# A planned order of all engines' work, replanned with a later landing of crossbar transposes, with new leads and offsets

## The chip, the cores and the metric

The kernel runs on one core of a Trainium2 chip. The metric is the device time of one execution in microseconds (us). Three runs of the kernel before took 236.09, 234.23 and 234.80 us, so the median is 234.80 us. A core has five engines that run side by side and each take their instructions in the order in which the program lists them: TensorE (PE, matrix products, with weight loads as PEld), VectorE (DVE), ScalarE (ACT), GpSimd (POOL) and SyncE (SP). POOL and SP compute nothing here: they issue transfers.

## The reference

For 8 batches of 576 positions, attention with 8 heads of 64 elements, in a sliding window of 128 positions with a linear position bias, and then a channel mix on its 512-wide result. In numpy, cut to what matters:

```python
scores = where((rel >= 0) & (rel < 128), q @ k.T / 8 - slope[h] * abs(rel), -1e9)
x = softmax(scores) @ v                       # heads side by side: (8, 576, 512)
x_prev = x shifted down by one position, zeros first
xk = mu_k * x + (1 - mu_k) * x_prev
xr = mu_r * x + (1 - mu_r) * x_prev
out = sigmoid(xr @ w_r) * (relu(xk @ w_k) ** 2 @ w_v)    # w_k 512x1024, w_v 1024x512
```

## The kernel before

**The work.** Positions lie in tiles of 128 (four and a half a batch), heads in four pairs g = 0 to 3. For every batch b and pair g the steps are:

- Transposed queries and keys. For batches 0 to 5 TensorE makes them (`qk_quad`, `qk_some`, lines 1053 and 804) and ScalarE or VectorE copies them out of PSUM (line 663). For batches 6 and 7 (`XB`) SyncE issues eight crossbar transposes for each batch (`flip`, line 502, tile `qx` from `cb`). The last 64 positions of batches 4 to 7 come by one more (`tail_flip`, line 595, `tt` from `ts`).
- Scores (`scores`, line 693, a contraction over 64 rows), the exponential on ScalarE (line 707, `at`), and the mask as a product on VectorE (line 720).
- Attention times values (`attend`, line 749, `duo`), the reciprocal of the sum (line 755) and the scaled result `xu` (line 760) on VectorE.
- The result transposed to `xt`: on TensorE for batches 0 to 5 (`out_t`, `out_some`, lines 787 and 804), by crossbar transposes from SyncE for batches 6 and 7 (`out_flip`, line 869, `xt` from `xu`).
- On VectorE the difference to the position before, `dl` (line 847), and the two mixtures `xk` and `xr` (line 854), in `shift`.

The channel mix then runs over groups of columns of two batches together, 512, 384 and 256 wide (`channel_mix`): eight products with `wk_sb` (line 958), each followed by a relu on ScalarE (line 965, `rl`) and a square on VectorE or ScalarE (lines 931 and 929, `kk`); and for each tile of 128 positions four matmuls with `wr_sb` (line 976), a tanh on ScalarE (line 983, `rs`), two halves of four matmuls with `wv_sb` (line 992), one VectorE instruction (line 997, `ot`), and a store from SyncE (line 1022). All of these, and the TensorE transposes, share four PSUM banks, `uno`; scores and most attention products use two double banks, `duo`.

**The order.** Nothing of the order is left to a scheduler at run time. The program describes every operation as a node with its engine, duration, delay to its followers, and the buffers it takes and gives back. `Plan.run` then plays all engines forward and, whenever an engine is free, gives it the ready node with the smallest key. The order that comes out is the order of the program. These constants feed it:

- `FLAT`: two delays of a crossbar transpose, between its issue and the start of its transfer, and from the end of its transfer to the time when its data may be used. `flip`, `tail_flip` and `out_flip` pass it on.
- `WAIT`: added to the key of a TensorE node marked lazy (transposes that use the array in halves of 64 rows) as long as the array is in its 128-row form.
- `LEAD` and `SHIFT`: an attention node's key is `(k - lead(e, k)) * SLOPE + SHIFT`, where k counts batches and pairs. `lead` interpolates the ten numbers of an engine, one for every fourth k. A larger lead puts the attention of that stretch earlier against the channel mix on that engine. A mix node's key is its own place plus a `SHIFT` by the buffers it takes and frees.

The four lines with the delay of a crossbar transpose, at the issue in `flip` and where the delays are used:

```python
        return dma(SPE, FLIP * RATE, FISSUE, lambda e: nc.sync.dma_start_transpose(
            ...
            [g, (cl[b][NF * i + j], FWAIT)], (), [ch[b]], FLAT, True)
        ...
        n0, edge = n, (n, lat[0])                       # in fab
            x = plan.add(FAB, us / m, lat[1] if i == m - 1 else 0.0, [edge], ...)
```

Of the kernel before, what the change touches and what calls it, by code (L numbers as in the profile page):

```python
# [182 lines left out]
def kernel(  # L183
# [29 lines left out]
    PE, ACT, DVE, POOL, SPE, FAB, VIR = "PE", "ACT", "DVE", "POOL", "SP", "FAB", "VIR"  # L213
# [15 lines left out]
    RUN = {2: 64 * 284 / 345.0, NF: 128 * 284 / 390.0}  # L229
    FLIP = 1.0  # L230
    FISSUE = 1.3
    FLAT = (0.4, 0.6)
    FWAIT = 6.0
    NO = 5
    WAIT = 3.32
    COST = {'first': 1.28, 'v': 1.15, 'q': 0.944, 'ts': 0.66, 'tv': 0.58, 'w': 0.88, 'run4': 1.0, 'run2': 1.03, 'flip': 1.0, 'mu': 1.0, 'x': 1.0}
    SS = ()
    OH = range(1, 6)
# [77 lines left out]
    def two(h):  # L316
# [3 lines left out]
                     xk=2, rl=3, kk=3, rs=4, ot=NO),  # L320
                {}, WAIT)
    LAT = {PE: 0.2, ACT: 0.22, DVE: 0.16}
# [7 lines left out]
    def dve_t(n, fast=1):  # L330
# [1 line left out]

    AHEAD = 30.0
    LEAD = {
        PE: (20.71, 45.98, 25.48, 22.48, 33.7, 13.57, 16.34, 19.02, 18.98, 21.49),
        ACT: (-12.8, -31.96, 26.95, -42.55, -38.86, -42.12, 50.62, -66.43, -27.26, -47.28),
        DVE: (-9.64, -23.6, -20.1, 21.59, -38.02, 19.17, 21.38, -10.6, -61.51, -15.57),
    }
    KNOTS = range(-4, 36, 4)
    SHIFT = {  # L340
        PE: {(0, 0): 75.8, (1, 0): 3.7, (2, 0): 53.98, (3, 0): 68.58, ('fkk',): -70.0, ('p1', 'fkk'): 14.4, ('p1', 'fxk'): 15.56},
        ACT: {(1, 0): -100.8, (2, 0): 67.78, (3, 0): 84.72, ('frl',): 15.27, ('rl', 'fp1'): 97.76, ('rs', 'fp1'): -101.33},
        DVE: {(0, 0): -161.9, (1, 0): 90.77, (1, 1): -32.45, (1, 2): -60.98, (2, 0): 28.48, (3, 0): -12.21, ('fp1', 'frs'): -33.9, ('frl',): -130.25, ('ot', 'fp1', 'frs'): -5.67},
    }
    NBIAS = 4
    XRL = 4.0
# [34 lines left out]
    def fab(queue, us, n, lat, free=(), flip=False):  # L381
        m = max(1, round(us / 0.25))
        us *= COST.get(getattr(n, "kind", None), 1.0)
        n0, edge = n, (n, lat[0])
        for i in range(m):
            x = plan.add(FAB, us / m, lat[1] if i == m - 1 else 0.0, [edge], (0,), None, (),
                         free if i == m - 1 else ())
            x.queue, x.base, x.flip = queue, n0, flip
            edge = (x, 0.0)
        return x  # L390
# [110 lines left out]
    def flip(b, i, j, g):  # L501
        return dma(SPE, FLIP * RATE, FISSUE, lambda e: nc.sync.dma_start_transpose(
            out=qx_buf[xbh[b].idx][:, i, :, 128 * j:128 * j + 128],
            in_=cb_buf[ch[b].idx][:, i, j].rearrange("p h d -> p (h d)")),
            [g, (cl[b][NF * i + j], FWAIT)], (), [ch[b]], FLAT, True)

# [84 lines left out]
    def tail_flip(b):  # L591
# [5 lines left out]
            in_=ts_buf[hs.idx].rearrange("p h d -> p (h d)")),  # L597
            [g] + [(x, FWAIT) for x in tl[b]], (), [hs], FLAT, True)]

# [266 lines left out]
    def out_flip(b, g, r, hx, ht):  # L866
# [4 lines left out]
            in_=xu_buf[hx.idx].rearrange("p t h d -> p (t h d)")))  # L871
        return [fab(SPE, FLIP * NJ / 4, n, FLAT, [hx], True)]

# [427 lines left out]
```

## Time and profile before

| | |
|---|---|
| median of three runs | 234.80 us |
| the profiled execution's own time | 233.99 us |
| its span, first to last instruction | 232.2 us |
| PE busy | 222.9 us, 96% |
| DVE busy | 187.7 us, 81% |
| ACT busy | 165.4 us, 71% |
| crossbar transposes `qx` from `cb` | 16, median 5.9 us from issue to landing |
| crossbar transposes `xt` from `xu` | 8, median 3.7 us |
| crossbar transposes `tt` from `ts` | 4, median 2.5 us |

The profile is of one execution. Its span is 1.8 us shorter than that execution's own time, which lies outside the first and the last instruction. The busy time of PE is the time in which at least one matmul is under way; matmuls follow each other before the one ahead has ended, so durations overlap, and the distance between the starts of two matmuls is what one costs.

### The profile page before, as it was taken

How to read it: one execution, taken by the hardware profiler on the slowest of the kernel's cores; microseconds unless marked ns; L12 is line 12 of the kernel's file. 1: busy time of each engine (PE TensorE's matmuls, PEld its weight loads, DVE VectorE, ACT ScalarE, POOL GpSimd, SP SyncE). 2: the span in 40 equal slices, each digit the busy share in tenths (PEclk: the TensorE clock that was granted, in tenths of full speed). 3: DMA queues.
4: the chain of work that ended last, by engine and by line, in shares of the span. 5: the costliest groups of instructions: out<-in, count | busy, mean ns of one | idle time of the engine just before them, and what ended most of it. 6: DMA issues, size and time to landing. Idle time of an engine off the chain costs nothing.

```text
span 232.2 us, 6668 instructions
## 1 busy us (share of the span) xinstructions
PE 222.9 (96%) x2687; PEld 135.2 (58%) x2715; DVE 187.7 (81%) x422; ACT 165.4 (71%) x296; POOL 93.9 (40%) x120
## 2 busy tenths in 40 slices
PE   8999799999999999999999999999998999999994
PEld 8676665765665755555665755555646644445462
DVE  7495899899868999879779997999989899624242
ACT  3769999699997985968998847478775636236261
POOL 8796654689977940097400992600000000000000
PEclk9999999999999999999999999999999999999999
DMA  7999999999999997089994999999412712121212
GB/s 171 184 167 193 187 170 199 204 165 178 168 165 146 168 156 139 0 96 173 211 149 113 153 143 194 142 183 197 54 51 90 110 54 74 47 91 45 93 45 90
DMA packets 121566, 31.11 MB, mean 134 GB/s; under 512 B 108216, under 2 KB 117696, under 8 KB 121536
## 3 DMA queue, kind: packets, MB, share of 16 engines
q0 software_dynamic: 96016, 16.26, 98.5%
q1 hardware_dynamic: 23776, 13.84, 26.2%
q10 hardware_dynamic: 1744, 0.59, 1.0%
q8 instruction: 21, 0.34, 0.7%
q14 instruction: 9, 0.07, 0.1%
HBM read 33.56 MB, written 9.44 MB: 185 GB/s over the span
## 4 chain that ended last, share of the span: by engine, by line
PE 74%; DVE 12%; DMA 7%; ACT 3%; issue 2%; POOL 1%; DVEq 0%; ACTq 0%
PE uno L992 22%; PE uno L958 20%; PE uno L976 11%; PE duo L749 6%; DMA wv_sb<-in_moe_w_v_dram 5%; PE duo L693 5%; PE uno L654 3%; PE uno L804 2%; DVE ot L997 2%; DMA xt<-xu 2%; DVE xr L854 2%; DVE dl L847 2%; DVE xk L854 2%; DVE at L720 2%; PE duo L680 1%
## 5 line engine op out<-in xcount | busy, mean ns | idle before, releaser
L992 PE MATMUL uno<-wv_sb,kk 128*128 128x512 bf16 (+2 forms) x277 | 70.4, 373 | 1.5 <-issue 0.3
L958 PE MATMUL uno<-xk,wk_sb 128*128 128x256 bf16 (+2 forms) x410 | 69.3, 313 | 0.9 <-ACT qk L663 0.4
L707 ACT ACTIVATE at<-duo 128x1024 bf16<-128x1024 f32 (+2 forms) x68 | 65.6, 1014 | 5.4 <-PE duo L693 5.3
L965 ACT ACTIVATE rl<-uno 128x256 bf16<-128x256 f32 (+2 forms) x104 | 48.1, 489 | 20.9 <-PE uno L958 16.5
L958 PEld LDWEIGHTS <-wk_sb 128*128 128x128 bf16 x416 | 38.4, 98 | 21.0 <-issue 1.6
L467 POOL DMA_DIRECT2D vs<-in_v_dram x32 | 28.4, 901 | 45.1 <-PE duo L749 37.9
L992 PEld LDWEIGHTS <-kk 128*128 128x128 bf16 x296 | 27.1, 98 | 29.5 <-issue 1.3
L720 DVE TENSOR_TENSOR at<-at,mask 128x1024 bf16<-128x1024 bf16 x56 | 37.0, 684 | 7.5 <-ACT at L707 7.3
L983 ACT ACTIVATE rs<-uno 128x512 bf16<-128x512 f32 x36 | 22.2, 624 | 24.5 <-PE uno L976 23.6
L976 PE MATMUL uno<-wr_sb,xr 128*128 128x512 bf16 x141 | 36.5, 379 | 1.1 <-DVE ot L997 0.9
L997 DVE SCALAR_TENSOR_TENSOR ot<-rs,uno 128x512 f32<-128x512 bf16 (+2 forms) x37 | 24.6, 667 | 15.3 <-PE uno L992 13.0
L931 DVE TENSOR_TENSOR kk<-rl 128x256 bf16<-128x256 bf16 (+2 forms) x96 | 31.0, 338 | 6.5 <-ACT rl L965 5.2
L663 ACT COPY qk<-uno 128x512 bf16<-128x512 bf16 (+1 forms) x42 | 22.8, 601 | 4.6 <-DVE rc L755 2.1
L854 DVE SCALAR_TENSOR_TENSOR xr<-dl,mu_sb,xt 128x576 bf16<-128x576 bf16 (+1 forms) x32 | 24.5, 775 | 0.0
L854 DVE SCALAR_TENSOR_TENSOR xk<-dl,mu_sb,xt 128x576 bf16<-128x576 bf16 (+1 forms) x32 | 24.3, 778 | 0.0
L749 PEld LDWEIGHTS <-at 128*128 128x128 bf16 x576 | 21.1, 98 | 5.1 <-issue 0.9
L976 PEld LDWEIGHTS <-xr 128*128 128x128 bf16 x144 | 13.9, 98 | 17.0 <-issue 0.9
L760 DVE TENSOR_TENSOR xu<-duo,rc 128x640 bf16<-128x640 f32 x28 | 22.5, 812 | 0.9 <-DMA xt<-xu 0.8
L498 POOL DMA_DIRECT2D cb<-in_k_dram x20 | 17.8, 920 | 2.6 <-DMA vs<-in_v_dram 1.6
L749 PE MATMUL duo<-vs,at 128*128 128x65 bf16 x448 | 18.7, 194 | 0.1
L498 POOL DMA_DIRECT2D cb<-in_q_dram x20 | 17.7, 922 | 1.4 <-PE uno L958 0.7
L663 ACT COPY xt<-uno 128x640 bf16<-128x640 bf16 (+3 forms) x28 | 15.0, 582 | 4.2 <-PE uno L804 2.8
(83 smaller groups left out, 201.3 us busy)
## 6 DMA issues: line engine op xcount, KB each, us to landing
out_dram<-ot SPq DMA_DIRECT2D x30, 256.0 KB, 4.5
vs<-in_v_dram POOLq DMA_DIRECT2D x32, 128.0 KB, 6.8
cb<-in_q_dram POOLq DMA_DIRECT2D x20, 128.0 KB, 6.3
cb<-in_k_dram POOLq DMA_DIRECT2D x20, 128.0 KB, 6.4
out_dram<-ot SPq DMA_DIRECT2D x10, 128.0 KB, 1.8
wk_sb<-in_moe_w_k_dram POOLq DMA_DIRECT2D x2, 512.0 KB, 7.4
cb<-in_q_dram POOLq DMA_DIRECT2D x4, 256.0 KB, 10.0
cb<-in_k_dram POOLq DMA_DIRECT2D x4, 256.0 KB, 10.3
```

What stands on the lines that cost most here:

```text
L498: return [dma(POOL, 256, issue_t(1024), lambda e, r=r: nc.gpsimd.dma_start(out=cb_buf[h.idx][:, i, r], in_=src[:, :, r]), [g], kind="q") f ...
L663: (nc.scalar.copy if e == ACT else nc.vector.tensor_copy)(out=out, in_=in_)
L707: lambda e, ah=ah, w=w, hp=hp: nc.scalar.activation(out=ah(), in_=two(hp)[:, :, 0:w], func=AF.Exp, scale=float(scale)), (), [hp])
L720: nc.vector.tensor_tensor(out=a, in0=a, in1=m, op=ALU.mult)
L749: nc.tensor.matmul(a[:, hl, t - t0], lhsT=at[:, lo:lo + 128], rhs=vs[:, u, 2 * g + hl, :] if u < NF else tvb[:, 2 * g + hl], start=(u == u ...
L854: lambda e: nc.vector.scalar_tensor_tensor(out=buf[hk.idx][:, g, e0 + c0:e0 + c1], in0=dls(), scalar=mu[:, g:g + 1], in1=xc(1), op0=ALU.mu ...
L931: nc.vector.tensor_tensor(out=out, in0=in_, in1=in_, op=ALU.mult)
L958: nc.tensor.matmul(one(hp)[:, 0:n], lhsT=wk_sb[:, po, 128 * fo:128 * fo + 128], rhs=xk_buf[hx.idx][:, po, c0:c1], start=(po == 0), stop=(p ...
L965: a = op(ACT, act_t(n), [s], pr, lambda e, hp=hp, hr=hr: nc.scalar.activation(out=rl_buf[hr.idx][:, 0:n], in_=one(hp)[:, 0:n], func=AF.Rel ...
L976: nc.tensor.matmul(one(hp), lhsT=xr_buf[hx.idx][:, po, 128 * c:128 * c + 128], rhs=wr_sb[:, po], start=(po == 0), stop=(po == NPO - 1))
L992: nc.tensor.matmul(one(hv)[:, a:b], lhsT=kk_buf[hk.idx][:, fo, o:o + 128], rhs=wv_sb[:, fo, a:b], start=(fo == 0), stop=(fo == NFO - 1))
L997: nc.vector.scalar_tensor_tensor(out=ot_buf[ho.idx][:, a:b], in0=rs_buf[hs.idx][:, a:b], scalar=1.0, in1=one(hv)[:, a:b], op0=ALU.add, op1 ...
```

## The change

Four sets of constants are replaced. The second delay in `FLAT` goes from 0.6 to 2.2 us, `WAIT` goes from 3.32 to 0.0, and the tables `LEAD` and `SHIFT` get new numbers. No function is changed, no operation is added or taken away, and the buffers are the same. The order in which `Plan.run` lists the operations of PE, ACT, DVE and SP is another. The order of POOL is the same.

```diff
-    FLAT = (0.4, 0.6)
+    FLAT = (0.4, 2.2)
     FWAIT = 6.0
     NO = 5
-    WAIT = 3.32
+    WAIT = 0.0
...
     LEAD = {
-        PE: (20.71, 45.98, 25.48, 22.48, 33.7, 13.57, 16.34, 19.02, 18.98, 21.49),
-        ACT: (-12.8, -31.96, 26.95, -42.55, -38.86, -42.12, 50.62, -66.43, -27.26, -47.28),
-        DVE: (-9.64, -23.6, -20.1, 21.59, -38.02, 19.17, 21.38, -10.6, -61.51, -15.57),
+        PE: (46.3, 80.42, 22.29, 25.79, 41.56, 20.38, 22.23, 21.29, 23.26, 26.51),
+        ACT: (-27.56, -45.55, 35.23, -5.26, -38.06, -61.17, 26.65, -81.7, -33.31, -34.13),
+        DVE: (-18.77, -31.64, -26.58, 23.63, -67.49, 40.6, 13.9, -0.29, -44.69, 6.99),
     }
...
     SHIFT = {
-        PE: {(0, 0): 75.8, (1, 0): 3.7, (2, 0): 53.98, (3, 0): 68.58, ('fkk',): -70.0, ('p1', 'fkk'): 14.4, ('p1', 'fxk'): 15.56},
-        ACT: {(1, 0): -100.8, (2, 0): 67.78, (3, 0): 84.72, ('frl',): 15.27, ('rl', 'fp1'): 97.76, ('rs', 'fp1'): -101.33},
-        DVE: {(0, 0): -161.9, (1, 0): 90.77, (1, 1): -32.45, (1, 2): -60.98, (2, 0): 28.48, (3, 0): -12.21, ('fp1', 'frs'): -33.9, ('frl',): -130.25, ('ot', 'fp1', 'frs'): -5.67},
+        PE: {(0, 0): 84.89, (1, 0): -15.49, (2, 0): 37.21, (3, 0): 68.05, ('fkk',): -41.42, ('p1', 'fkk'): 6.29, ('p1', 'fxk'): 4.19},
+        ACT: {(1, 0): -163.12, (2, 0): 31.31, (3, 0): 165.14, ('frl',): 21.61, ('rl', 'fp1'): 159.69, ('rs', 'fp1'): -160.42},
+        DVE: {(0, 0): -143.93, (1, 0): 53.57, (1, 1): -50.21, (1, 2): -15.35, (2, 0): 32.09, (3, 0): -4.67, ('fp1', 'frs'): -48.4, ('frl',): -99.03, ('ot', 'fp1', 'frs'): -1.01},
     }
```

## Prediction

> **What bounds the kernel now.** I read the page first, then the waits of PE, then the order of time around each wait.
>
> ```profile
> PE 222.9 (96%) x2687; PEld 135.2 (58%) x2715; DVE 187.7 (81%) x422; ACT 165.4 (71%) x296; POOL 93.9 (40%) x120
> ...
> PEclk9999999999999999999999999999999999999999
> ...
> PE 74%; DVE 12%; DMA 7%; ACT 3%; issue 2%; POOL 1%; DVEq 0%; ACTq 0%
> ```
>
> PE is busy for 96% of the span, at full granted clock in each slice, and is three quarters of the chain that ended last. Whether a busy PE is a full PE is told by the starts of its matmuls, in the timeline of PE (start, duration, line, shapes, count):
>
> ```profile
> 154.63 1.03 PE L976 MATMUL uno<-wr_sb,xr 128*128 128x512 bf16 x4
> 155.49 1.03 PE L992 MATMUL uno<-wv_sb,kk 128*128 128x512 bf16 x4
> 156.45 0.56 PE L693 MATMUL duo<-qx 64*128 64x256 bf16 x8
> 156.85 0.19 PE L693 MATMUL duo<-tt,qx 64*128 64x64 bf16 x2
> 156.88 0.19 PE L693 MATMUL duo<-tt 64*128 64x64 bf16 x2
> 157.00 1.04 PE L992 MATMUL uno<-wv_sb,kk 128*128 128x512 bf16 x4
> ```
>
> Four matmuls 512 wide take 0.86 us (155.49 less 154.63), 0.216 each, and the next four follow at once: this stretch is full. The four ahead of the scores take 0.96: the change to the 64-row form costs 0.10 us, and the change back about as much (0.12 us for two matmuls that cost some 0.03 together). In the sum a change costs 0.095.
>
> What PE waits for, in the view of its waits (us in total, times, longest):
>
> ```profile
> PE uno L879 <- ACT qk L663: 1.2, 1, 1.2
> PE uno L654 <- DVE warm L434: 1.0, 1, 1.0
> PE uno L976 <- DVE ot L997: 0.9, 1, 0.9
> PE uno L958 <- ACT qk L663: 0.4, 1, 0.4
> ```
>
> By the timeline the first, second and fourth lie ahead of 45 us. The third, at 175 us, is the only long one behind that. The rest there is short: 0.1 to 0.15 us each, about 0.4 in all. It matters where they lie because, by the orders of the two programs, PE lists the same instructions until about 47 us; up to there ACT and DVE each exchange two neighbours. So the change can win back some 1.3 us of waits between 47 us and the last matmul at 229.2, and no more. The 3.0 us from there to the end of the span, the last VectorE step and the stores, have the same operations in both.
>
> **The wait that goes.** In the timelines of DVE and PE:
>
> ```profile
> 169.18 0.46 DVE L847 TENSOR_TENSOR dl<-xt 128x576 bf16<-128x576 bf16 x1 [0.98 <-DMA xt<-xu]
> ...
> 174.65 0.68 DVE L997 SCALAR_TENSOR_TENSOR ot<-rs,uno 128x512 f32<-128x512 bf16 x1
> ```
>
> ```profile
> 175.38 1.02 PE L976 MATMUL uno<-wr_sb,xr 128*128 128x512 bf16 x4 [0.88 <-DVE ot L997]
> ```
>
> DVE stood 0.98 us for a crossbar transpose of batch 6, with all its later work behind it; 6 us later L997 gave a bank back late, and PE stood 0.88 us. What covers such a transpose is the DVE work listed between the multiplication that makes `xu` (L760) and the subtraction that reads `xt` (L847). Counted for the eight transposes with the rows' distances (L720, L997 0.60; L760, L854 0.73; L847 0.37; L931 0.21 to 0.33; L755 0.13 to 0.2), it is 5.1, 3.6, 5.4, 4.6, 3.3, 8.0, 7.0 and 3.9 us before, and 5.6, 7.3, 4.9, 12.6, 5.3, 5.9, 5.0 and 6.3 after. The transposes land in 2.4 to 4.9 us, median 3.7. The second, with 3.6 us of cover, is the one that was late (4.5). After, the least cover is 4.9. So the wait goes: **-0.88 us**. What is late next there is PE itself: the rows of L958 follow.
>
> **What is added.** The operations and their durations are the same, so PE's sum changes only by changes of form. Counted in the two orders there are 98 before and 102 after (lazy transposes no longer wait for 3.32 in the key): 4 x 0.095 = **+0.38 us**, all on the path. Matmul work, warm-up included, is 222.2 us before and 222.6 after. The Trainium skill has a rule for this, in "TensorEngine Tiling (Array Packing)": a change of tiling mode, not of tile, drains the array. The trace agrees, with 0.10 us a change; the page gives no price, and by it too the new order is the dearer one.
>
> The order on ACT and DVE costs nothing where PE has other work ahead of what waits for it. At the end it has: 40.7 us of matmul work after the last attention product, 38.1 before, and between that product and the first L958 that needs its mixtures 16.4 us in both, against some 8 us for L755, L760, transpose, L847 and four L854. The exchange on ACT near 17 us (an exponential ahead of a 0.3 us copy) is made good by the next instruction: nothing.
>
> **What is brought nearer.** The first scores of batch 7 have 161.5 us of matmul work ahead before and 155.5 after: six us earlier. They started at 166.64, so 5.1 us were lost by then. They read `qx`, all eight transposes, and `tt`. SP's timeline before (its queue in order), and the landings of `qx`:
>
> ```profile
> 138.41 11.50 SPq L502 DMA_TRANSPOSE qx<-cb  x7
> 150.75 0.34 SPq L1022 DMA_DIRECT2D out_dram<-ot  x1
> 151.18 1.30 SPq L502 DMA_TRANSPOSE qx<-cb  x1
> 152.65 1.24 SPq L595 DMA_TRANSPOSE tt<-ts  x1
> ```
>
> ```profile
> DMA to landing us min/median/max: 2.5/5.6/8.2
> ```
>
> The last `qx` was issued at 151.2 and landed by 159.4 at the latest, 7 us ahead of need. After, SP lists one transpose, then a store, then seven, then `tt`. That store's mix has 136.0 us of matmul work up to its end. The two stores ahead of the transposes before had 129.5 and 132.1 and were issued at 137.4 and 138.0, 5.9 to 7.9 us later on the clock. So the store goes at 141.8 to 143.8. Seven transposes at the row's 1.64 us: the last starts at 151.7 to 153.7 and lands, at the median, at 157.3 to 159.3, at the worst at 161.9; `tt` is issued at 153.3 to 155.3 and lands with its own 2.5 us by 157.8, with the worst of `qx` by 163.5. Needed: 155.5 + 5.1 = 160.6. The cost is between nothing and 2.9 us. I take nothing, as the medians stay 1.3 us clear. What waits behind the scores, if they are late, is all of PE.
>
> For batch 6 the same count (scores at 130.4 + 4.9 = 135.3; the six transposes behind the store with 105.5 us start near 112, and are through by 121) leaves over 6 us.
>
> **The sum.** 233.99 (the profiled execution: span 232.2 and 1.8 around it) - 0.88 + 0.38 = 233.5. The shown runs have a median 0.8 us above this execution; from them the sum is 234.3. I take the middle, **233.9 us**. One per cent, 2.35 us, is about what a measurement of this kernel can tell from no change.
>
> **The rivals.**
> 1. *The transposes of batch 7 come too late* (slower than before). Place: the first L693 of batch 7. It decides when the last of them lands more than 160.6 us into the span. For it: `qx` took up to 8.2 us beside the loads, 2.5 at the least, and in the new order the last attention product of batch 5, for which POOL's loads of `vs` wait, comes 3.5 us of work later, so these loads fall on the transposes. Against it: the earlier loads, of `cb`, come 1.8 us sooner, and the median is clear. Price up to 2.9: 233.5 + 2.9 = 236.4, from the runs' median 237.2; with half of it 235. The Trainium skill, "DMA: Bandwidth & Descriptors", on queue arbitration, has each DMA engine go round between queues packet by packet, which is how loads would stretch a transpose; the spread of 2.5 to 8.2 agrees. Chance 0.2.
> 2. *The wait only changes its place.* The halves of L992 are parted in 36 of 38 tiles in both orders, and hold one of four banks, but after they are parted by other things than L976 (L958, L749, L693), so banks come free in another rhythm. If as much is lost as in the wait that goes, +0.38 remains: 234.4 to 235.2. This is also the case in which the change does not do what it says. For it: DVE is busy for 19.0 of the 20 us from 160. Against it: the larger covers. Chance 0.22.
> 3. *More goes than the 0.88.* The three runs are 1.9 us apart, and covers of 3.3 and 3.6 us against landings up to 4.9 would cost more in an execution with slower transposes. If all 1.3 us go, 233.1 in this execution, and the median falls to it. Chance 0.15.
>
> **How the numbers follow.** My forecast has 0.43. Range: from rival 3, less 0.4 for the runs' spread, 232.7, to rival 1 from both starting points, 236.8. Slower by over 1% (237.15) needs rival 1 at its full price on the slower runs, or several small waits: 0.15. Faster by over 1% (232.45) needs more than all the waits there are: 0.07. Within 1%: 0.78.
>
> **What would show it.** Right: no wait of `dl` for `xt` on DVE over 0.3 us; no PE wait for L997 near 175; PE busy about 0.4 us up; the last matmul near 228.7. Wrong: an idle stretch of PE ahead of the first L693 with `qx` and `tt` of batch 7 near 160.6, ended by SP's transposes; or waits of L958, L976 or L992 for L965, L983 or L997 that sum to over 1 us. The prediction fails as a whole if the first 47 us, which list nearly the same, do not take the same time.

## The result, and the profile after

The kernel after takes 232.56 us, the median of 15 runs (231.68 to 234.98). The kernel before took 235.14 us in 15 runs beside them (234.09 to 238.11). The ratio is 0.9897, with a 95% interval of 0.9869 to 0.9925: about 1% faster. The ratios are formed from the fast runs alone (a few executions take some per cent longer at a lower granted clock), the medians from all runs, so a ratio is not exactly the quotient of two medians. The forecast was 233.9 us from a start of 234.8, a ratio of 0.996. Its direction is right. Its size is less than half of what was measured, and the median lies 0.14 us below the lower end of the range.

The two profiled executions stand closer together: 233.99 us before and 232.61 us after, spans of 232.2 and 230.8 us. That is 1.38 us, where the medians are 2.58 us apart. Both differences have to be explained.

The page of the kernel after, its busy times, its granted clock and the shares of the chain that ended last:

```profile
PE 221.1 (96%) x2682; PEld 134.3 (58%) x2715; DVE 186.9 (81%) x422; ACT 163.9 (71%) x296; POOL 93.7 (41%) x120
...
PEclk9999999999999999999999999999999999999999
...
PE 77%; DMA 16%; issue 2%; POOL 2%; DVE 1%; ACT 1%; DVEq 0%; POOLq 0%; ACTq 0%
```

DVE fell from 12% to 1% of the chain. Some 15 of these 27 us lay between 159 and 192 us, in the chain before from `xt<-xu` over DVE to PE, and they are gone; the other 12 lay ahead of 55 us, where the chain after takes another way. The waits of PE after (us in total, times, longest):

```profile
PE uno L654 <- DVE warm L434: 1.0, 1, 1.0
PE uno L992 <- issue: 0.8, 5, 0.2
PE uno L992 <- DMA wv_sb<-in_moe_w_v_dram: 0.7, 1, 0.7
PE duo L680 <- ACT at L707: 0.5, 1, 0.5
```

The row of L976 waiting for L997 is no longer there, and the waits over 0.2 us lie ahead of 45 us. DVE no longer waits for a transpose of `xt` either: its list of waits has no such row. The landings of the eight transposes, in the rows of tile `xt`, were 2.4, 3.7 and 4.9 us at the least, median and most before, and are after:

```profile
DMA to landing us min/median/max: 2.4/2.4/3.8
```

**Where the time went.** The waits view leaves out what is below 0.15 us or lies inside a group. So I count PE's delay in another way. For each weight load of the trace I take its start, less the matmul work that the program lists ahead of it. The work is the number of matmuls times the distance of their starts in a full stretch (0.216 us for 512 columns, 0.162 for 384, 0.109 for 256, 0.029 for 65, and 0.095 for each change of form). The result is what PE has lost so far:

| us of matmul work done | before | after | FLAT alone | tables alone | before, no `xt` transposes |
|---|---|---|---|---|---|
| 49 | 3.52 | 3.92 | 4.18 | 4.04 | 5.51 |
| 161 | 4.86 | 4.48 | 5.52 | 4.61 | 6.80 |
| 198 | 6.42 | 4.38 | 5.52 | 4.51 | 6.80 |
| 222 (end) | 6.78 | 4.54 | 5.88 | 4.67 | 7.15 |

(The last three columns are experiments, below.) Read down a column, this tells in which stretch time is lost. From 161 to 198 us of work, which is 166 to 204 us on the clock and where the transposes of `xt` run, before lost **1.56 us** and after nothing. The difference of the profiled pair is then:

- the start, up to 49 us: +0.40. No effect of the change can be read from it: PE's order is the same up to 47.6 us on the clock, and the executions profiled in the order of before have between 3.1 and 5.5 there;
- from 49 to 161: 0.56 in place of 1.34, so -0.78;
- the stretch of the transposes: -0.10 in place of 1.56, so -1.66;
- the last 24 us: 0.16 in place of 0.36, so -0.20;
- four more changes of form: +0.38;
- from the fourth weight load from the end (228.76 and 226.90 us; an expectation below calls it the last) to the end of the span, 3.44 us before and 3.94 after: +0.49.

The sum is -1.37 us, and the spans differ by as much. Ahead of the transposes the new order thus won 0.78 us, which no run takes apart further, and it paid about as much in changes of form and at the end (0.38 and 0.49).

### The profile page after: what moved, and what is told of

The parts are those of the page before. It is cut to its first block, busy times and chain, and to the rows that moved or that the text cites. A ratio compares the mean times of both kernels' runs of the same rounds, so it can differ in the third digit from the quotient of the medians.

```text
span 230.8 us, 6660 instructions
## 1 busy us (share of the span) xinstructions
PE 221.1 (96%) x2682; PEld 134.3 (58%) x2715; DVE 186.9 (81%) x422; ACT 163.9 (71%) x296; POOL 93.7 (41%) x120
## 4 chain that ended last, share of the span: by engine, by line
PE 77%; DMA 16%; issue 2%; POOL 2%; DVE 1%; ACT 1%; DVEq 0%; POOLq 0%; ACTq 0%
PE uno L992 25%; PE uno L958 25%; PE uno L976 12%; DMA wk_sb<-in_moe_w_k_dram 7%; PE duo L749 6%; PE duo L693 5%; DMA cb<-in_k_dram 5%; DMA vs<-in_v_dram 4%; PE uno L804 3%; POOL vs L467 1%; PE uno L1053 0%; DVE dl L847 0%; POOL tv L472 0%; PE uno L879 0%; ACT xt L663 0%
## 5 line engine op out<-in xcount | busy, mean ns | idle before, releaser
L958 PE MATMUL uno<-xk,wk_sb 128*128 128x256 bf16 (+2 forms) x413 | 70.8, 313 | 0.6 <-ACT qk L663 0.4
L992 PE MATMUL uno<-wv_sb,kk 128*128 128x512 bf16 (+2 forms) x282 | 69.5, 373 | 1.9 <-issue 0.8
L965 ACT ACTIVATE rl<-uno 128x256 bf16<-128x256 f32 (+2 forms) x104 | 47.4, 487 | 30.2 <-PE uno L958 27.0
L720 DVE TENSOR_TENSOR at<-at,mask 128x1024 bf16<-128x1024 bf16 x56 | 37.3, 681 | 3.4 <-ACT at L707 3.4
L997 DVE SCALAR_TENSOR_TENSOR ot<-rs,uno 128x512 f32<-128x512 bf16 (+2 forms) x37 | 24.4, 667 | 13.8 <-PE uno L992 10.3
L976 PE MATMUL uno<-wr_sb,xr 128*128 128x512 bf16 x128 | 34.3, 379 | 0.8
L760 DVE TENSOR_TENSOR xu<-duo,rc 128x640 bf16<-128x640 f32 x28 | 22.5, 813 | 2.1 <-PE uno L804 2.1
L976 PEld LDWEIGHTS <-xr 128*128 128x128 bf16 x144 | 13.6, 98 | 14.2 <-issue 0.2
```

The lines of the kernel that those rows point to most:

```text
L720: nc.vector.tensor_tensor(out=a, in0=a, in1=m, op=ALU.mult)
L958: nc.tensor.matmul(one(hp)[:, 0:n], lhsT=wk_sb[:, po, 128 * fo:128 * fo + 128], rhs=xk_buf[hx.idx][:, po, c0:c1], start=(po == 0), stop=(p ...
L965: a = op(ACT, act_t(n), [s], pr, lambda e, hp=hp, hr=hr: nc.scalar.activation(out=rl_buf[hr.idx][:, 0:n], in_=one(hp)[:, 0:n], func=AF.Rel ...
L976: nc.tensor.matmul(one(hp), lhsT=xr_buf[hx.idx][:, po, 128 * c:128 * c + 128], rhs=wr_sb[:, po], start=(po == 0), stop=(po == NPO - 1))
L992: nc.tensor.matmul(one(hv)[:, a:b], lhsT=kk_buf[hk.idx][:, fo, o:o + 128], rhs=wv_sb[:, fo, a:b], start=(fo == 0), stop=(fo == NFO - 1))
```

## The experiments

The theory (called A) was that the transposes of `xt` for batches 6 and 7, late in some places, hold DVE, which works in order, and through it PE, and that this is what the change removes. Its rivals were that the gain lies elsewhere, in the new order of PE and its banks, and (D) that the narrow margin of batch 7's transposes costs something after.

### The transposes left out, in both orders

Everything stays in its place, but SP does not issue the eight transposes; batches 6 and 7 are mixed from what stands in the buffer, so that part of the computation is left out.

```diff
-                      lambda e: nc.sync.dma_start_transpose(out=xt_buf[...], in_=xu_buf[...]))
+                      lambda e: None)
```

> The kernel before in its own order on every engine, without the eight crossbar transposes of xt from xu in batches 6 and 7 (line 869): that part of the computation is left out, so xt holds what batches 4 and 5 left there. Theory A, the late crossbar transposes are the cause: the matmul delay that before builds up from 163 to 194 us of its span (1.7 us by the start of its weight loads against the matmul work ahead of them) goes, and the time falls by 1.5 to 2.5 us, to that of the changed kernel within 0.5 us. Theory B, the gain is from the rhythm of banks and buffers in the new order: the time falls by less than 0.5 us, as DVE still does all its work in the old order.

> The changed kernel in its own order, also without the eight transposes of xt from xu (left out as in the run beside it). Theory A: nothing in it waits for them, so the time stays that of the changed kernel within 0.4 us. Theory B says the same here. If it falls by 1 us or more, the new order is still held up by them.

Before without them took 233.48 us (232.95 to 234.36), a ratio of 0.9887 [0.9845, 0.9929] to before on the same chip. After without them took 233.43 us, 0.9881 [0.9836, 0.9927]. The fall before, 2.8 us by the medians, is a little more than the 2.5 at most that was expected. Without the transposes the two orders are equal within the intervals, and they have the ratio that the change has with them (0.9897). Before loses about 1.1% to them, after nothing that can be measured. The table's last column shows where: the loss between 161 and 198 is gone. This settles the place of the cause. It also bounds what the rest of the new order is worth by itself: nothing that these runs resolve.

### Each transpose issued twice

```diff
+        def emit_f(e):
+            for _ in range(2):
+                nc.sync.dma_start_transpose(out=xt_buf[...], in_=xu_buf[...])
```

> The kernel before in its own order, each transpose of xt from xu issued twice to the same place, the second behind the landing of the first, so that the data of each is there 2.4 to 4 us later. Nothing is left out. Theory A: with the least covers 3.3, 3.6 and 3.9 us on DVE against landings of 5 to 8 us, the time rises by 3 to 6 us. Theory B: by less than 1 us.

> The changed kernel in its own order, each transpose of xt from xu issued twice as in the run beside it. Theory A: with the least covers 4.9 to 5.6 us the time rises too, but by 1 to 2.5 us less than before does. Theory B: by as little as in before.

Before rose to 246.29 us (1.0418 [1.0351, 1.0485]), after to 244.97 us (1.0381 [1.0323, 1.044]). Both expectations failed: before lost 10 us where 3 to 6 had been expected, and the two orders lost nearly the same (their intervals overlap). The reason stands in SP's queue. The second transpose has the same destination and waits for the landing of the first, with all later transfers of SP behind it. In the order of before the first was issued at 156.12 us and landed at 164.53, and the second was issued at 164.55 and landed at 166.98; in the order of after the first landed at 161.87, and the second was issued at 161.89. What followed in the order of before, in the timelines of DVE, ACT and PE (the lines of `channel_mix` stand three lower in this file: L934 is the square, L968 the relu, L961 the products with `wk_sb`):

```profile
167.07 0.46 DVE L847 TENSOR_TENSOR dl<-xt 128x576 bf16<-128x576 bf16 x1 [5.86 <-DMA xt<-xu]
```

```profile
168.49 0.87 ACT L968 ACTIVATE rl<-uno 128x384 bf16<-128x384 f32 x2 [5.96 <-DVE kk L934]
```

```profile
169.04 5.41 PE L961 MATMUL uno<-xk,wk_sb 128*128 128x384 bf16 x20 [5.55 <-ACT rl L968]
```

The transpose holds `dl`, and with it the squares that stand behind it on DVE; the relus wait for a square, and PE for a relu. So the wait goes on to PE whole, within 2 us. Neither order has cover for that much (DVE's longest wait for `xt` was 5.9 us in the old order and 5.2 in the new), so this pair does not tell the orders apart. It needed a smaller dose.

### One more transpose ahead of each, to a spare tile

```diff
+    spare = cst.tile([128, 4, 640], BF16, name="spare")
...
+            for dst in (spare[:, g], xt_buf[...]):
+                nc.sync.dma_start_transpose(out=dst, in_=xu_buf[...])
```

> The kernel before in its own order, with one more crossbar transpose ahead of each transpose of xt, of the same data to a tile that nothing reads, not waited for: each landing comes 1.2 to 1.5 us later, and SP is held no longer than that. Nothing is left out. Theory A: least covers of 3.3 to 3.9 us against landings of 3.7 to 6.4, so 2 to 5 us slower than before.

> The changed kernel in its own order with the same additional transposes. Theory A: least covers of 4.9 us and above, so slower than the changed kernel by 1.5 us at most, and still faster than before, ratio below 1.0. Theory B: it loses as much as before does.

Before with it took 238.8 us (236.97 to 239.85), 1.0114 [1.0054, 1.0174]. After with it took 234.9 us (233.97 to 236.97), 0.9986 [0.9944, 1.0028] of before: some 0.9% over the plain kernel after, more than expected, and its ratio below 1 is not resolved. The same delay of every transpose thus costs some 3.5 us in the old order by the medians, and some 2.2 in the new one (234.9, less the 232.7 of the new order in the same comparison, with tables alone). By the ratios it is 1.1% and 0.9%, so the runs do not resolve that the new order loses less. The profiles show where it does, in one execution each, of which that of the old order (239.77 us) is near its slowest. Between 148 and 198 us of work, where the transposes run, PE lost 7.9 us in the old order (1.7 without the addition) and 2.5 in the new (nothing without it). DVE's waits in the old order and then in the new (L848 here is L847 of the kernel before):

```profile
DVE dl L848 <- DMA xt<-xu: 4.7, 3, 3.1
```

```profile
DVE dl L848 <- DMA xt<-xu: 2.3, 2, 1.8
```

With L761, which waits for the transposes too (1.8 and 1.3 us), it is 6.5 and 3.6 us: in these executions the new order waits about half as long for the same delay. That fits theory A and more cover; that the new order is more robust in time stays unproven.

### One part of the change alone

First FLAT alone, in the kernel before:

```diff
-    FLAT = (0.4, 0.6)
+    FLAT = (0.4, 2.2)
```

> The kernel before with the one constant FLAT at (0.4, 2.2), the tables and WAIT as before, planned anew. The VectorE work listed between a product xu and the subtraction that reads its transpose becomes 6.1, 5.5, 7.6, 4.4, 5.3, 4.3, 9.4 and 0.9 us for the eight (before 5.1, 3.6, 5.4, 4.6, 3.3, 8.0, 7.0, 3.9); the last one has 16 us of matmul work ahead of who needs it. Theory A, the cover of the transposes is the gain: 1.5 to 2.5 us faster than before. Theory B, the searched tables are what gains: less than 0.8 us faster, or slower, as the old tables were searched for the old delay.

Then the new tables alone, which is the kernel after with FLAT put back:

```diff
-    FLAT = (0.4, 2.2)
+    FLAT = (0.4, 0.6)
```

> The changed kernel with FLAT back at (0.4, 0.6), its new tables kept, planned anew. The covers become 5.6, 7.3, 14.7, 3.4, 5.3, 2.9, 4.3 and 3.9 us. Theory A: three covers are below the 4 to 5 us of a slow landing again, so 0.5 to 1.5 us of the gain is lost. Theory B: the time stays that of the changed kernel within 0.4 us, a ratio near 0.99 to before.

FLAT alone took 233.37 us (232.42 to 234.93), 0.9899 [0.9857, 0.9942]. The tables alone took 232.7 us, 0.9857 [0.982, 0.9895]. Each has the gain of the whole change within the intervals (the tables' 0.9857 is 0.989 by the medians). FLAT alone does one thing in the table above: the 1.56 us between 161 and 198 become 0.00, and the 1.34 ahead of it stays as in before. That is the same cure as leaving the transposes out, by one constant. PE lists the same matmuls as before up to 179 us on the clock there, so the wait at 175 us goes without any change of PE's own order.

For the tables alone I had expected a loss of 0.5 to 1.5 us, because the DVE work that covers the eight transposes is then 5.6, 7.3, 14.7, 3.4, 5.3, 2.9, 4.3 and 3.9 us. Nothing was lost, and DVE has no wait for `xt`. The landings in that run tell why; the rows of tile `xt`:

```profile
DMA to landing us min/median/max: 2.4/2.4/4.3
```

By the single transfers, the longest two (2.94 and 4.33 us) are the first two, which have 5.6 and 7.3 us of cover, and those with 2.9 to 4.3 us of cover landed in 2.4. Before it was the other way round: the second landed in 4.49 us and had 3.6 of cover. So the least cover by itself says little. What counts is each transpose's own cover against its own landing.

WAIT was not run alone, for there is nothing to run: with it the planner lists the same program on every engine as before. And the new tables with the old WAIT have the 102 changes of form as well.

### The kernel after again, and the last transpose of batch 7 left out

> The changed kernel as it is, on the same chip as the three runs beside it. Both theories: ratio to before 0.987 to 0.993; its spread is narrower than that of before.

```diff
-        ... lambda e: nc.sync.dma_start_transpose(
+        ... lambda e: b == 7 or nc.sync.dma_start_transpose(
```

The `tt` transpose of batch 7 is left out, and with it the last 64 positions of that batch are computed from what stands in the buffer.

> The changed kernel in its own order, without the one crossbar transpose of tt from ts of batch 7 (line 595; this part of the computation is left out). In the changed kernel's profile it landed at 160.19 us and its matmuls started at 160.35. Theory C, this narrow margin costs time in the slower executions: median lower by 0.5 to 1 us and no execution above 233.5. Theory D, it does not: within 0.4 us of the changed kernel.

The kernel after took 232.66 us (232.17 to 232.82), 0.99 [0.9876, 0.9924]. Without the transpose it took 232.53 us (231.7 to 233.35), 0.989 [0.986, 0.992]. So this transfer costs nothing that the runs resolve, though it comes with hardly any time to spare. In the profile of the kernel after `tt` was issued at 152.28 us, and the longest landing in the rows of tile `tt` belongs to it:

```profile
DMA to landing us min/median/max: 2.5/5.2/7.9
```

It landed at 160.19. PE's timeline there:

```profile
159.00 1.03 PE L992 MATMUL uno<-wv_sb,kk 128*128 128x512 bf16 x4
159.96 0.56 PE L693 MATMUL duo<-qx 64*128 64x256 bf16 x8
160.35 0.19 PE L693 MATMUL duo<-tt,qx 64*128 64x64 bf16 x2
160.38 0.19 PE L693 MATMUL duo<-tt 64*128 64x64 bf16 x2
160.74 0.81 PE L992 MATMUL uno<-wv_sb,kk 128*128 128x512 bf16 x3 [0.16 <-issue]
```

The first matmul that reads `tt` starts at 160.35, 0.16 us behind the landing, where it would start anyway: 0.39 us behind the eight scores, against 0.40 in the stretch that the prediction showed. The 0.16 us of the last row is no wait for it: the record of one of the four matmuls of that half is missing.

### The tail

The tail is longer after. The last three stores on SP (start, time of the three issues) follow each other closely, and the last of them had its data ready some 0.4 us before SP issued it at 227.96 (the VectorE step ended at 227.54). The store of the tile before last is cut in two. This edit moves the cut one tile ahead, so that that store goes in one piece:

```diff
-  cut = (a, 256, b) if 0 < B * S - 128 - row <= 128 * n_split else (a, b)
+  cut = (a, 256, b) if 128 < B * S - 128 - row <= 128 * (n_split + 1) else (a, b)
```

> The changed kernel with the store of the tile of positions before the last one issued in one piece of 512 columns; an earlier tile is split in two in its place, so the number of transfers stays. In the changed kernel's profile the last store waits on SP behind the two halves and is issued at 227.96 us, 0.5 us after its data. If that is why the stretch from the last weight load to the end grew from 3.45 to 3.94 us, it shrinks to 3.5 or less, and the time by 0.3 to 0.5 us. If the new order of the matmuls at the end is the reason in itself, nothing changes.

With FLAT put back too:

> The same change of the last stores on the order planned with the new tables and FLAT at (0.4, 0.6). If the two gains add up: ratio to before 0.982 to 0.988, the fastest of the four. If the old FLAT was ahead of the changed kernel by chance of the runs: as the run with the changed stores, within 0.3 us.

The stores on SP in the timeline of the kernel after, and then with that edit:

```profile
227.06 1.31 SPq L1022 DMA_DIRECT2D out_dram<-ot  x3
```

```profile
227.11 0.85 SPq L1022 DMA_DIRECT2D out_dram<-ot  x2
```

One issue less is in that row, and the time from the fourth weight load from the end falls from 3.94 to 3.75 us, not to the 3.5 that was expected. In the time this can't be told: 232.49 us (231.64 to 236.62), 0.9892 [0.9863, 0.9922]. With the old FLAT as well it is 232.57 us, 0.9905 [0.9879, 0.993], so the 0.9857 of the tables alone did not come back, and these gains do not add. No version is shown to be faster than the kernel after.

## Why the prediction was right in direction and short in size

**What was right.** The kernel is bound by PE; the wait that goes is the one at 175 us with its cause, the second transpose of batch 6; the covers after (least 4.9 us) are above the longest landing (3.8 us). Both signs named for it came: no wait of `dl` for `xt`, no PE wait for L997.

**The term of -0.88 was too small.** This step failed. The prediction took the one wait on PE's list as all that late transposes cost. The stretch lost 1.56 us in the same execution, and 1.66 us were won there. Set beside the run without the transposes, which has the same order, the loss comes in two parts: 0.9 us at 175.38, the wait on the list, and some 0.6 us at 188.9, 190.1 and 192.5. Ahead of the second part DVE stood for a transpose once more:

```profile
183.20 0.82 DVE L760 TENSOR_TENSOR xu<-duo,rc 128x640 bf16<-128x640 f32 x1 [0.81 <-DMA xt<-xu]
...
188.21 0.68 DVE L997 SCALAR_TENSOR_TENSOR ot<-rs,uno 128x512 f32<-128x512 bf16 x1
188.80 1.29 DVE L720 TENSOR_TENSOR at<-at,mask 128x1024 bf16<-128x1024 bf16 x2
```

L760 writes the `xu` buffer that the fourth transpose (issued at 179.35, landed at 183.11) still read. The prediction counted cover only up to L847, which reads the result, and not up to the instruction that needs the source buffer again; this row stood in DVE's waits before (0.8 us). From there DVE works without a gap until 191.3, and PE follows it:

```profile
187.01 1.03 PE L976 MATMUL uno<-wr_sb,xr 128*128 128x512 bf16 x4
187.88 1.03 PE L992 MATMUL uno<-wv_sb,kk 128*128 128x512 bf16 x4
188.94 1.02 PE L958 MATMUL uno<-xk,wk_sb 128*128 128x512 bf16 x4
189.80 0.77 PE L749 MATMUL duo<-vs,at 128*128 128x65 bf16 x15
190.41 0.19 PE L749 MATMUL duo<-tv,at 128*128 128x65 bf16 x1
```

Four matmuls cost 0.86 us between 187.01 and 187.88, and 1.06 between 187.88 and 188.94, with no wait in brackets; L997 ends at 188.89. The fifteen at 189.80 take 0.61 up to the next one, where the fifteen at 177.10 take 0.46; the masks of L720 end at 190.09. This is 0.35 us of loss within 3 us, and the list shows none of it. At 192.5 PE goes on behind a relu of 191.86, which had waited for DVE's square of 191.34. That this part goes with the transposes is shown (it is gone without them); that it comes from the hold at 183.20 is read from these rows and was not tried by itself. The bound that followed from the list, "some 1.3 us of waits between 47 us and the last matmul at 229.2, and no more", was wrong for the same reason: 3.26 us were lost there (6.78 less 3.52), of which after has 0.62 left.

**The start was a lucky execution.** The profiled execution of before, 233.99 us, is nearly the fastest: the lowest of 54 runs of that kernel is 233.91. The profiled execution of after, 232.61, is at its median. The 2.58 us between the medians beside the 1.38 of the profiled pair may then be transposes that land later in other executions of before. The spreads speak for it only in part: without the transposes the same order stays within 1.4 us in six runs, and the kernel after within 0.65 us in the six of its repetition, where the runs of before that enter the same comparisons reach from 233.91 to 237.24 us; but the 15 runs of after in the result reach over 3.3 us too, and the six of after without the transposes over 2.4. That the transposes cost 1.1% by the medians is shown (they were left out); that they do it by later landings in those executions is argued, since only one execution of before was profiled. The prediction saw this as rival 3, "covers of 3.3 and 3.6 us against landings up to 4.9 would cost more in an execution with slower transposes", gave it 0.15, and capped it at 1.3 us by the bound above. The middle of 233.5 and 234.3 that it forecast instead had no mechanism behind it.

**The last 3 us were costed at nothing** because they have the same operations. They cost +0.49, with the stores issued in a tighter row; one store less in that row won 0.19 of it back.

**The changes of form** stay at +0.38 by count and price. No run measured them alone. Their cause was told wrongly: the four more come with the tables, not with WAIT, which changes nothing by itself. And the sign "PE busy about 0.4 us up" was a bad sign: it fell from 222.9 to 221.1, though there is more work: busy time also holds small delays between matmuls whose durations overlap in the view, and these became fewer. The last matmul ended at 227.3, not near 228.7. The prediction would have failed as a whole, by its own words, if the first 47 us did not take the same time; they differ by some 0.4 us, less than executions of the same order do.

**Rival 1** did not come, but closer than was said. `qx` went nearly as reckoned: the last was issued at 150.90, 0.8 us ahead of the range, and landed at 158.04. For `tt` the prediction took "its own 2.5 us" from the two landings before that the trace has, of transposes issued at 90.62 and 124.49 us, when POOL issued no loads; that of batch 7 is not among them. After, it took 7.9 us, in a stretch where POOL's loads run. The margin was 0.16 us and not 2.8 to 4.8. The runs without it show that 0.16 was enough. **Rival 2** fell: the waits did not come back in another place, as nothing is lost after 161 us of work.

**Chances.** A ratio of 0.9897 is just past the 1% that "faster" was given 0.07 for. That small chance rested on the bound of 1.3 us alone.

## What to carry to other kernels

When one engine is busy for 96%, count what it has lost by the start of its instructions less the work listed ahead of them; the list of its waits held only 0.88 of the 1.56 us that late transfers cost. Compare the own time of the profiled execution with the spread of the runs before starting the sum from it: if it is at the fast end, a cause that varies from run to run costs more in the median than in the trace. For a transfer that an in-order engine waits for, set the work that covers it against its own landing, one by one, both for the instruction that reads the result and for the one that reuses the source buffer, and take the landing from a row with the same neighbours.

## What was not expected of the hardware

**A wait of PE under 3 us was followed by half the clock.** In the profiled execution with the spare transposes in the old order PE waited 2.76 us, up to 165.86. By stretches of its time (us, length, PE busy and matmuls, granted clock, DMA share, GB/s):

```profile
160.00:163.00 3.00, 3.00 (x48) 1.00 1.30 222
163.00:166.00 3.00, 0.24 (x5) 1.00 0.50 184
166.00:168.00 2.00, 2.00 (x10) 0.68 0.00 0
168.00:170.00 2.00, 2.00 (x8) 0.50 0.46 103
170.00:172.00 2.00, 2.00 (x21) 0.97 1.14 69
```

The clock fell to 0.50 when PE was already at work again, and stayed for some 3.5 us. The twenty matmuls of 384 columns behind the wait took 5.03 us (165.86 to 170.89) in place of 20 x 0.162 = 3.24, so the wait of 2.8 us cost 4.5. With each transpose issued twice in the old order the twenty took 5.34 us behind a wait of 5.55; there the clock had fallen during the wait. In the new order with the spare transposes a wait of 1.6 us left the clock at full. The Trainium skill, "TensorE: Matmul & The Clock Gate", Part 1, has half rate after at least one idle window of about 3.4 us. The trace agrees with the half rate, and not with the length: here 2.8 us without a matmul were enough. A late transfer can thus have a price that jumps: 1.8 of the 7.9 us that PE lost in that execution are the half clock. The other three runs of that kernel have mean clocks of 0.998 to 1.000, against 0.993 in this one.

**The landing of a crossbar transpose between two buffers on the chip** took 2.4 us for `xt` at the least, also with the next one issued 1.3 us behind it (after, at 169.56 and 170.94), and up to 6.1 us with FLAT alone and 8.4 us with each transpose issued twice, there for the first of them, at 156 us. For `qx` it was up to 9.8 us (before, without the transposes of `xt`). Why the second `xt` of before took 4.49 us, and the same one with FLAT alone 2.39, was not settled: in before the next transpose was issued 1.3 us behind it, with FLAT alone 2.9 us, but with the tables alone one took 4.33 us with 5.6 us of room.
